# Reordering the input products of two chained MLPs by their weight tiles, with block 0's products cut in two

## The chip, the cores and the metric

The kernel runs on one core of a Trainium2 chip. The metric is the device time of one execution in microseconds (us). Before the change it is 1236.48 us, the median of three runs (1236.11 to 1237.58).

## What is computed

The reference chains three stages over 8192 tokens of width 192: a causal window of 7 neighbours weighted by a softmax, an MLP with SiLU, and an MLP with a rational activation. The changed code is in the first product of each MLP, `h = x @ w_in`.

```python
def _moe_ref(x, w_in, w_out):
    h = x @ w_in                              # 8192x192 by 192x2048
    g = h * (1.0 / (1.0 + np.exp(-h)))
    return (g @ w_out).astype(np.float32)

def _moe2_ref(x, w_in, w_out, a, b):
    h = x @ w_in
    h2 = h * h
    h3 = h2 * h
    P = a[0] + a[1] * h + a[2] * h2 + a[3] * h3
    Q = 1.0 + np.abs(b[0]) * np.abs(h) + np.abs(b[1]) * h2
    g = P / (Q + 1e-06)
    return (g @ w_out).astype(np.float32)
```

## The kernel before

The tokens are handled in 16 blocks `b` of 512 columns. `attention(b)` (line 530) makes the block's input on VectorE (DVE) and GpSimd (POOL), TensorE (PE) transposes it into PSUM, and `split_x` (line 650) splits it into a high and a low part in fp32r: ScalarE (ACT) writes `xh` (line 655), and after it DVE writes `xl` (line 659) as what `xh` left over. Those two steps stand in the plan as `XH0`, `XL0` for the first MLP and `XH1`, `XL1` for the second, whose input is the first one's accumulator (`between`, line 739).

Weights are split in the same way: `WA` holds the first 128 rows of `w_in` as a high and a low tile, `WB` the other 64 rows with high above low. `mm1` (line 667) makes one unit `u` of `h`: two tiles of 128 hidden features (`i` is 0 or 1), each from five products of a 128x128 weight tile with 512 columns of `xh` or `xl`. There are 8 units for each block and MLP, called `A0` to `A7` in the first MLP and `B0` to `B7` in the second, so 256 units and 2560 products. `mm2` (line 691) adds a unit's activation into the accumulator with ten products more (`C0` to `C7`, `D0` to `D7`).

In `mm1` the order is by moving operand: first the three products with `xh` for `i` = 0 and the three for `i` = 1, then the two with `xl` for `i` = 0 and the two for `i` = 1. So the first product that needs `xl` is the seventh of ten.

The order of all steps is a table written by hand (`ORDER`): each engine takes its steps in the order in which they stand there, and a step's engine waits at a single instruction until what it reads has been written. After `mm1`, ACT reads the whole `h` (SiLU in line 723, the linear part in line 768, the magnitude in line 772), so it waits for the last product of a unit. The buffer of `h` is one of four PSUM pairs, marked A to D in the table, and is free for the next unit when the last reader of the former one has ended.

At the start PE runs two warm-up steps without a result: `W0` (line 636) transposes the same 128x128 piece of `xw` 84 times, and `W1` (line 614) the same piece of `ao` 16 times.

Of the kernel before, what the change touches and what calls it, by code (L numbers as in the profile page):

```python
# [20 lines left out]
P = 128  # L21
# [3 lines left out]
BT = JB * P  # L25
# [195 lines left out]
SHARED = {"y", "t", "g1h", "g1l", "g2h", "g2l", "ao", "of", "xh0", "xl0", "xh1", "xl1", "pr"}  # L221
BANKS = {"h", "acc0", "acc1", "dec"}
OWN = dict(xw=1, aw=2)
CHUNKS = (4, 4, 8, 16, 16, 16)
WARM = (84, 16)

# [48 lines left out]
def kernel(  # L275
# [13 lines left out]
    pe, act, dve, pool, sp = nc.tensor, nc.scalar, nc.vector, nc.gpsimd, nc.sync  # L289
# [29 lines left out]
    def new(buf, shape, dt=F32, name=None):  # L319
        if buf[0] in SHARED:  # L320
            return sb.tile(shape, dt, tag="s" + plan.slot[buf], name=name or buf[0], bufs=1)
        return sb.tile(shape, dt, tag=buf[0], name=name or buf[0], bufs=OWN[buf[0]])

    def bank(buf, shape=(P, 2, BT), name=None):
        return ps.tile(list(shape), F32, tag="p" + plan.slot[buf], name=name or buf[0], bufs=1)
# [339 lines left out]
    def mm1(m, b, u):  # L665
        hb = ("h", m, b, u)
        xh, xl = (f"xh{m}", b), (f"xl{m}", b)

        def run(e):
            if hb not in st:  # L670
                st[hb] = bank(hb)
            h, th, tl = st[hb], st[xh], st[xl]
            first = ((WA[m][0], th[:, 0]), (WA[m][1], th[:, 0]), (WB[m], th[:, 1]))
            second = ((WA[m][0], tl[:, 0]), (WB[m], tl[:, 1]))
            for terms in (first, second):
                for i in range(2):
                    f = slice((2 * u + i) * P, (2 * u + i + 1) * P)
                    for n, (w, xx) in enumerate(terms):
                        pe.matmul(  # L679
                            out=h[:, i], lhsT=w[:, f], rhs=xx,  # L680
                            start=(terms is first and n == 0), stop=(terms is second and n == 1),
                        )

        first = [(*hb, 0)] if (m, b, u) == (0, 0, 0) else []
        plan.op(
            f"{'AB'[m]}{u}", b, "PE", run, rd=[*first, (*xh, 0), (*xl, 0), ("W", m, "A", u // 4), ("W", m, "B", u // 4)],
            wr=[(*hb, 0)],
        )
        return hb
# [202 lines left out]
    for m in range(2):  # L892
        for u in range(NU):
# [4 lines left out]
            if u % 2 == 0:  # L898
                weights(m, "O", u // 2)
    for i in range(2, len(CHUNKS)):  # L900
        softmax(f"s{i}", sum(CHUNKS[:i]), CHUNKS[i], False)
    for b in range(NB):
# [43 lines left out]
```

## Time and profile before

| | before |
|---|---|
| median of three runs | 1236.48 us (1236.11 to 1237.58) |
| span of the profiled execution | 1234.3 us |
| outside that span (median less span) | 2.2 us |
| PE, matmuls | 1210.9 us busy, 98% |
| PE, weight loads (PEld) | 1000.2 us busy, 81% |
| ACT | 1107.3 us busy, 90% |
| DVE | 1060.1 us busy, 86% |
| POOL | 704.4 us busy, 57% |

The profile gives no time of its own for the profiled execution beside its span; the 2.2 us are the median of the runs less that span. In the timeline a row has its start and its length in us, the engine, the line of the kernel, the operation, the output and the inputs, and how many instructions it merges; in brackets stands how long the engine sat idle before it and what ended that. Matmuls overlap: a matmul's row is longer than the distance to the next one's start, and this distance, not the length, is what one costs in a stream.

### The profile page before, as it was taken

The numbers are of one execution on the slowest core, as the hardware profiler recorded it, in microseconds if no ns is written. First come the engines' busy times: TensorE is split into PE (matmuls) and PEld (weight loads), VectorE is DVE, ScalarE is ACT, GpSimd is POOL, SyncE is SP. The second block draws the span as 40 slices with busy tenths as digits, with TensorE's granted clock in tenths as the row PEclk, the third lists the DMA queues.
The fourth block names the chain that finished last, engine by engine and source line by source line (L and its number), as shares of the span: only waits on it lengthen the run. The fifth ranks groups of instructions, "written<-read, shape, count | busy, mean of one in ns | idle before, by whom it ended". The sixth has DMA issues, their size and how long they took to land.

```text
span 1234.3 us, 14596 instructions
## 1 busy us (share of the span) xinstructions
PE 1210.9 (98%) x5476; PEld 1000.2 (81%) x5476; DVE 1060.1 (86%) x956; ACT 1107.3 (90%) x1053; POOL 704.4 (57%) x455
## 2 busy tenths in 40 slices
PE   6999999999999999999999999999999999999998
PEld 5777888888888888888888888888888888888786
DVE  8899899898799887898899998787887888878797
ACT  4999999889899999798987998988999899999996
POOL 3758578777654656657446773756727454241531
PEclk8999999999999999999999999999999999999999
DMA  8810010110010100100001020100101000000000
GB/s 245 254 60 33 9 64 9 36 37 25 33 37 3 61 18 1 58 32 25 15 1 54 13 64 1 31 31 1 57 1 54 2 13 9 5 22 1 9 14 26
DMA packets 19230, 45.15 MB, mean 37 GB/s; under 512 B 3932, under 2 KB 10714, under 8 KB 19160
## 3 DMA queue, kind: packets, MB, share of 16 engines
q1 hardware_dynamic: 19160, 44.22, 11.5%
q8 instruction: 43, 0.70, 0.2%
q14 instruction: 27, 0.22, 0.1%
HBM read 31.73 MB, written 7.90 MB: 32 GB/s over the span
## 4 chain that ended last, share of the span: by engine, by line
PE 86%; DVE 6%; ACT 5%; issue 2%; DMA 1%; POOL 1%; SPq 0%; ACTq 0%; DVEq 0%; POOLq 0%
PE h L679 43%; PE acc L710 8%; PE acc L711 8%; PE acc L706 8%; PE acc L708 8%; PE acc L707 8%; ACT L911 1%; PE to L835 1%; DVE y L787 1%; DVE g1l L731 1%; ACT y L792 1%; ACT y L795 1%; ACT y L772 1%; DVE dec L461 1%; DVE t L778 1%
## 5 line engine op out<-in xcount | busy, mean ns | idle before, releaser
L808 POOL TENSOR_TENSOR g2l<-t,g2h 128x1024 fp32r<-128x1024 f32 x95 | 247.5, 2612 | 162.7 <-DVE g2h L317 93.2
L679 PE MATMUL h<-xh,wa 128*128 128x512 f32 x1024 | 317.6, 391 | 4.2 <-DVE g1l L731 1.8
L315 POOL TENSOR_SCALAR g2h<-t 128x1024 fp32r<-128x1024 f32 x84 | 108.8, 1298 | 230.6 <-DVE t L798 207.4
L679 PEld LDWEIGHTS h<-xh,wa 128*128 128x128 f32 x1024 | 190.6, 188 | 48.6 <-issue 3.8
L911 ACT ACT_TABLE_LOAD x167 | 214.3, 1283 | 3.7 <-PEq L930 0.7
L787 DVE SCALAR_TENSOR_TENSOR y<-y,b_sb 128x1024 f32<-128x1024 f32 x128 | 184.6, 1450 | 23.0 <-ACT y L772 22.7
L679 PE MATMUL h<-xl,wa 128*128 128x512 f32 x512 | 199.4, 390 | 0.4 <-DVE xl L659 0.4
L679 PE MATMUL h<-xh,wb 128*128 128x512 f32 x512 | 199.3, 389 | 0.0
L679 PE MATMUL h<-xl,wb 128*128 128x512 f32 x512 | 199.3, 389 | 0.0
L731 DVE TENSOR_TENSOR g1l<-h,g1h 128x1024 fp32r<-128x1024 f32 x128 | 155.6, 1219 | 47.8 <-ACT g1h L727 43.5
L778 DVE TENSOR_TENSOR t<-t,h 128x1024 f32<-128x1024 f32 x128 | 155.2, 1214 | 40.1 <-ACT t L768 26.2
L798 DVE SCALAR_TENSOR_TENSOR t<-t,a_sb,y 128x1024 f32<-128x1024 f32 x128 | 174.3, 1376 | 16.3 <-ACT y L795 16.0
L581 POOL TENSOR_TENSOR pr<-xw,aw 128x768 f32<-128x768 f32 (+1 forms) x99 | 153.0, 1554 | 32.2 <-DMA aw<-wsm 10.9
L781 DVE SCALAR_TENSOR_TENSOR t<-t,a_sb,h 128x1024 f32<-128x1024 f32 x128 | 163.5, 1278 | 8.2 <-ACT y L772 4.9
L723 ACT ACTIVATE h<-h 128x1024 f32<-128x1024 f32 x128 | 129.5, 1012 | 40.2 <-PE h L679 35.0
L768 ACT ACTIVATE t<-h,a_sb 128x1024 f32<-128x1024 f32 x128 | 153.4, 1202 | 13.1 <-PE h L679 12.0
L772 ACT ACTIVATE y<-h,b_sb 128x1024 f32<-128x1024 f32 x128 | 141.9, 1112 | 19.6 <-PE h L679 13.7
L792 ACT ACTIVATE y<-y,c_sb 128x1024 f32<-128x1024 f32 x128 | 144.4, 1148 | 10.4 <-DVE y L787 9.7
L727 ACT ACTIVATE g1h<-h 128x1024 fp32r<-128x1024 f32 x128 | 131.0, 1027 | 6.4 <-PE acc L711 1.3
L795 ACT ACTIVATE y<-y 128x1024 f32<-128x1024 f32 x128 | 131.1, 1054 | 0.6
L679 PEld LDWEIGHTS h<-xl,wa 128*128 128x128 f32 x512 | 96.1, 188 | 20.9 <-DVE xl L659 0.9
L679 PEld LDWEIGHTS h<-xh,wb 128*128 128x128 f32 x512 | 96.2, 188 | 20.3
(96 smaller groups left out, 2249.9 us busy)
## 6 DMA issues: line engine op xcount, KB each, us to landing
xw<-in_x_dram SPq DMA_DIRECT2D x14, 960.0 KB, 4.8
raw<-in_moe_w_out_dram SPq DMA_DIRECT2D x16, 383.5 KB, 7.2
out_dram<-of SPq DMA_DIRECT2D x15, 384.0 KB, 2.6
e<-e SPq DMA_DIRECT2D x32, 128.0 KB, 2.3
raw<-in_moe_w_in_dram SPq DMA_DIRECT2D x8, 511.8 KB, 7.3
raw<-in_moe_w_in_dram SPq DMA_DIRECT2D x8, 255.9 KB, 7.6
aw<-wsm SPq DMA_DIRECT2D x14, 112.0 KB, 3.1
sm<-in_weight_gen_dram SPq DMA_DIRECT2D x3, 448.0 KB, 3.8
```

The source lines that it names most:

```text
L581: e.tensor_tensor(out=p.rearrange("p k (h g) -> p k h g", g=G), in0=st[xw][:, j + k0:j + k0 + n, :].rearrange("p k (h g) -> p k h g", g=G) ...
L679: pe.matmul(out=h[:, i], lhsT=w[:, f], rhs=xx, start=(terms is first and n == 0), stop=(terms is second and n == 1),)
L731: dve.tensor_tensor(out=t, in0=st[hb], in1=st[gh].bitcast(F32), op=ALU.subtract)
L768: act.activation(out=q, in_=st[hb], func=AF.Identity, scale=a_sb[:, 3:4], bias=a_sb[:, 2:3])
L772: act.activation(out=q, in_=st[hb], func=AF.Abs, scale=b_sb[:, 1:2])
L778: dve.tensor_tensor(out=st[t], in0=st[t], in1=flat(), op=ALU.mult)
L781: dve.scalar_tensor_tensor(out=st[t], in0=st[t], scalar=a_sb[:, 1:2], in1=flat(), op0=ALU.add, op1=ALU.mult)
L787: dve.scalar_tensor_tensor(out=st[y], in0=st[y], scalar=b_sb[:, 0:1], in1=st[y], op0=ALU.add, op1=ALU.mult)
L792: act.activation(out=st[y], in_=st[y], func=AF.Ln, scale=c_sb[:, 0:1], bias=1e-6)
L798: dve.scalar_tensor_tensor(out=st[t], in0=st[t], scalar=a_sb[:, 0:1], in1=st[y], op0=ALU.add, op1=ALU.mult)
L808: e.tensor_tensor(out=q, in0=st[t], in1=st[gh].bitcast(F32), op=ALU.subtract)
L911: act.preload_act_table((None, AF.Silu, AF.Ln, AF.Sigmoid, AF.Exp)[k])
```

## The change

Per tile `i` the five products now run in one go, in the order `WA` high with `xh`, `WA` high with `xl`, `WA` low with `xh`, `WB` with `xh`, `WB` with `xl`. The second and the fifth have the weights of the one ahead. In block 0 each product is cut into two of 256 columns, one behind the other with the same weights.

```diff
+PARTS = ((slice(0, BT),), (slice(0, BT // 2), slice(BT // 2, BT)))
...
             first = ((WA[m][0], th[:, 0]), (WA[m][1], th[:, 0]), (WB[m], th[:, 1]))
             second = ((WA[m][0], tl[:, 0]), (WB[m], tl[:, 1]))
-            for terms in (first, second):
-                for i in range(2):
-                    f = slice((2 * u + i) * P, (2 * u + i + 1) * P)
-                    for n, (w, xx) in enumerate(terms):
-                        pe.matmul(
-                            out=h[:, i], lhsT=w[:, f], rhs=xx,
-                            start=(terms is first and n == 0), stop=(terms is second and n == 1),
-                        )
+            terms = (first[0], second[0], first[1], first[2], second[1])
+            for i in range(2):
+                f = slice((2 * u + i) * P, (2 * u + i + 1) * P)
+                for n, (w, xx) in enumerate(terms):
+                    for c in PARTS[b == 0]:
+                        pe.matmul(out=h[:, i, c], lhsT=w[:, f], rhs=xx[:, c], start=(n == 0 and c.start == 0), stop=(n == 4 and c.stop == BT))
```

On PE, unit `B2` of block 8 (the first of the second MLP in that block) stood so before; `wa_73` is the high tile, `wa_74` the low one:

```order
L679 MATMUL h<-xh_5273,wa_73 128x512
L679 MATMUL h<-xh_5273,wa_74 128x512
L679 MATMUL h<-xh_5273,wb_76 128x512
L679 MATMUL h<-xh_5273,wa_73 128x512
L679 MATMUL h<-xh_5273,wa_74 128x512
L679 MATMUL h<-xh_5273,wb_76 128x512
L679 MATMUL h<-xl_5294,wa_73 128x512
L679 MATMUL h<-xl_5294,wb_76 128x512
```

The last two rows come once more, for the second tile. With the change the same place reads:

```order
L681 MATMUL h<-xh_5433,wa_73 128x512
L681 MATMUL h<-xl_5454,wa_73 128x512
L681 MATMUL h<-xh_5433,wa_74 128x512
L681 MATMUL h<-xh_5433,wb_76 128x512
L681 MATMUL h<-xl_5454,wb_76 128x512
```

These five come twice. The first product that reads `xl` moved from the seventh place to the second.

In block 0, unit `A0` now reads, also on PE:

```order
L681 MATMUL h<-xh_284,wa_71 128x256 x2
L681 MATMUL h<-xl_313,wa_71 128x256 x2
L681 MATMUL h<-xh_284,wa_72 128x256 x2
L681 MATMUL h<-xh_284,wb_75 128x256 x2
L681 MATMUL h<-xl_313,wb_75 128x256 x2
```

Where ten products of 512 columns stood there are twenty of 256. No row on the other engines moves.

## Rows read from the trace of the kernel before

**Rows 1.** The page's first part: busy time, share of the span and instructions of each engine.

```profile
PE 1210.9 (98%) x5476; PEld 1000.2 (81%) x5476; DVE 1060.1 (86%) x956; ACT 1107.3 (90%) x1053; POOL 704.4 (57%) x455
```

**Rows 2.** The page's fourth part: the chain that ended last, by engine and by line.

```profile
PE 86%; DVE 6%; ACT 5%; issue 2%; DMA 1%; POOL 1%; SPq 0%; ACTq 0%; DVEq 0%; POOLq 0%
PE h L679 43%; PE acc L710 8%; PE acc L711 8%; PE acc L706 8%; PE acc L708 8%; PE acc L707 8%; ACT L911 1%; PE to L835 1%; DVE y L787 1%; DVE g1l L731 1%; ACT y L792 1%; ACT y L795 1%; ACT y L772 1%; DVE dec L461 1%; DVE t L778 1%
```

**Rows 3.** Busy time by stretch: us, then PE, PEld, DVE, ACT, POOL, clock, DMA.

```profile
28.00:122.00 94.00, 90.43 (x395) 72.09 (x395) 87.69 (x104) 88.72 (x99) 66.47 (x49) 0.99 0.37 119
122.00:1165.00 1043.00, 1042.74 (x4701) 863.25 (x4699) 889.14 (x764) 948.45 (x885) 607.46 (x380) 1.00 0.08 24
1165.00:1235.00 70.00, 62.01 (x280) 49.98 (x278) 60.77 (x58) 58.33 (x56) 20.24 (x10) 0.99 0.07 21
```

**Rows 4.** Who PE waited for from 30 to 122 us: total, times, longest.

```profile
PE h L679 <- ACT xh L655: 0.6, 1, 0.6
PE h L679 <- DVE wa L482: 0.5, 1, 0.5
```

**Rows 5.** Timeline of PE in the middle of the run.

```profile
605.79 0.39 PE L679 MATMUL h<-xh,wb 128*128 128x512 f32 x1
606.02 0.39 PE L679 MATMUL h<-xl,wa 128*128 128x512 f32 x1
```

**Rows 6.** Timeline of the weight loads in the same place.

```profile
605.80 0.19 PEld L679 LDWEIGHTS h<-xl,wa 128*128 128x128 f32 x1
```

**Rows 7.** Groups of instructions by line: step `W0`.

```profile
L636 PE MATMUL tp<-ident,xw 128*128 128x128 f32 x84 | 11.4, 307 | 8.0 <-DMA xw<-in_x_dram 8.0
L636 PEld LDWEIGHTS tp<-ident,xw 128*128 128x128 f32 x84 | 11.2, 162 | 8.0 <-issue 8.0
```

**Rows 8.** Timeline of PE, the later part of `W0`.

```profile
13.81 5.40 PE L636 MATMUL tp<-ident,xw 128*128 128x128 f32 x48
```

**Rows 9.** Timeline of PE: eight transposes of eight different tiles.

```profile
175.71 1.03 PE L835 MATMUL to<-ident,of 128*128 128x128 f32 x8
```

**Rows 10.** Timeline of the weight loads behind an idle stretch of PE.

```profile
177.01 0.30 PEld L679 LDWEIGHTS h<-xh,wa 128*128 128x128 f32 x2 [0.50 <-DVE g1l L731]
```

**Rows 11.** Timeline of DVE and PE, unit `A2` of block 1.

```profile
68.97 1.22 DVE L659 TENSOR_TENSOR xl<-tp,xh 128x1024 fp32r<-128x1024 f32 x1
...
70.25 0.50 PE L679 MATMUL h<-xl,wa 128*128 128x512 f32 x1 [0.45 <-DVE xl L659]
70.59 0.40 PE L679 MATMUL h<-xl,wb 128*128 128x512 f32 x1
```

**Rows 12.** Timeline of DVE and PE, unit `B2` of block 8.

```profile
662.92 1.21 DVE L659 TENSOR_TENSOR xl<-acc,xh 128x1024 fp32r<-128x1024 f32 x1
...
663.17 0.62 PE L679 MATMUL h<-xh,wa 128*128 128x512 f32 x2
```

**Rows 13.** Timeline of DVE and PE, unit `B0` of block 10.

```profile
802.36 1.23 DVE L659 TENSOR_TENSOR xl<-acc,xh 128x1024 fp32r<-128x1024 f32 x1 [0.29 <-ACT xh L655]
...
802.93 0.62 PE L679 MATMUL h<-xh,wa 128*128 128x512 f32 x2
```

**Rows 14.** Timeline of DVE and PE, unit `B2` of block 15.

```profile
1173.09 1.23 DVE L659 TENSOR_TENSOR xl<-acc,xh 128x1024 fp32r<-128x1024 f32 x1
...
1173.11 0.73 PE L679 MATMUL h<-xh,wa 128*128 128x512 f32 x2 [0.76 <-ACT xh L655]
1173.68 0.40 PE L679 MATMUL h<-xh,wb 128*128 128x512 f32 x1
```

**Rows 15.** Timeline of DVE and PE, unit `B0` of block 2.

```profile
211.01 1.21 DVE L659 TENSOR_TENSOR xl<-acc,xh 128x1024 fp32r<-128x1024 f32 x1
...
212.04 0.61 PE L679 MATMUL h<-xh,wa 128*128 128x512 f32 x2
```

**Rows 16.** Timeline of DVE and PE, unit `A1` of block 12.

```profile
873.59 1.22 DVE L659 TENSOR_TENSOR xl<-tp,xh 128x1024 fp32r<-128x1024 f32 x1
...
874.98 0.67 PE L679 MATMUL h<-xh,wa 128*128 128x512 f32 x2
```

## The prediction

> **What bounds the kernel now.** I read the page's first part, then the chain of waits, then busy time by stretch, and last the timelines at the places that the change touches. The first part shows PE at 98%, with ACT and DVE at 90% and 86% [rows 1]; the chain has 86% on PE, 43% of it on `mm1`'s line alone [rows 2]. By stretch this is sharper: from 122 to 1165 us PE is busy for 1042.74 of 1043 us [rows 3]. There it waits for nobody, so whatever lengthens or shortens its stream does so to the end, with no gap to take it up. Before 122 us and after 1165 us PE has gaps: 3.6 us of 94, and 8.0 us of 70 [rows 3].
>
> What one product costs is the distance between starts: 605.79 to 606.02 us, so 0.23 us [rows 5]. I take 0.227, as 1042.74 us over 4701 matmuls with a few transposes among them is near it [rows 3]. Its weight load begins with the start of the product ahead, at 605.80, and has 0.19 us on its row [rows 6]: each load is hidden under the product before it.
>
> **Part 1: repeated weights.** Outside block 0 there are 240 units with four repeats each, 960 products. Do they get cheaper? The nearest row is `W0`, whose 84 transposes all have one and the same 128x128 weight tile. They show 84 loads for 84 matmuls [rows 7], so there a repeat loads again. In its later part 48 of them take 5.40 us; less the last one's own length of about 0.27 that is 5.13 / 47 = 0.109 us each [rows 8]. Eight transposes of eight different tiles take (1.03 - 0.27) / 7 = 0.109 us each [rows 9]. A repeat is neither skipped nor faster. Those are plain fp32 tiles of 128 columns and the products here are fp32r tiles of 512, so this is not proof, but it is the nearest row there is. And since a 512-column product hides its load anyway, a load that became shorter would save nothing by itself. **Taken: 0 us.** Ends: nothing, or the 13 ns of the rival below.
>
> **Part 2: `xl` is needed five places earlier.** Only the first unit of a block and MLP can notice, 32 places. Before, PE had six products (1.36 us) of `xh` ahead of the first one with `xl`; now it has one. The price of a late `xl` follows from unit `A2` of block 1, the one place where PE waits for `xl` already: DVE ends at 68.97 + 1.22 = 70.19, PE's row begins at 70.25, and it is 0.50 long where 0.39 is usual, because its own load could not run ahead [rows 11]. So a late `xl` starts PE's stream again 0.06 + 0.11 = 0.17 us after DVE's end. Place by place, DVE's end + 0.17 against the time at which the second product would have started (the first's start + 0.227):
>
> - `B2`, block 8: 664.13 + 0.17 = 664.30 against 663.40: 0.90 us [rows 12].
> - `B0`, block 10: 803.59 + 0.17 = 803.76 against 803.16: 0.60 us [rows 13].
> - `B0`, block 2: 212.22 + 0.17 = 212.39 against 212.27: 0.12 us [rows 15]. `B0` of block 7 reads alike, 0.12 us.
> - `B2`, block 15: 1174.32 + 0.17 = 1174.49 against about 1173.45 (the first product starts late after a wait, and the third's row at 1173.68 is 0.23 behind the second): 1.04 us [rows 14].
> - `A2`, block 1: PE waits until 70.25 before and after; then it had four products left and now has nine, 5 x 0.227 = 1.13 us [rows 11].
>
> At the other 26 `xl` ends before the load of the second product is issued (the closest is `A1` of block 12: 873.59 + 1.22 = 874.81 against 874.98 [rows 16]), or, in block 0, inside the first pair of products.
>
> The four in the saturated stretch, 0.90 + 0.60 + 0.12 + 0.12 = **1.74 us**, count in full. Behind each, the rest of the unit, ACT's step on it and all of PE's queue come later. The two in the stretches with gaps, 1.13 + 1.04 = 2.17 us, I count at half, **1.09 us**: PE's later gaps there are waits for DVE, ACT and POOL, which in part run on `h` themselves and so come later too. Ends of this part: 0, if DVE catches up, and 3.9 us.
>
> **Part 3: block 0 in halves.** 16 units with ten products make 160 pairs of 256 columns where 160 products of 512 stood. The trace has no 256-column product. The lower end is the 0.109 us of a 128-column matmul [rows 9]: two cost 0.218, less than 0.227, so 160 x -0.009 = -1.4 us. The upper end is a straight line between 128 and 512 columns, 0.109 + (0.227 - 0.109) / 3 = 0.148, so 0.296 a pair and 160 x 0.069 = +11 us. Which is nearer is decided by the load, since every half loads again: behind an idle stretch two loads of this very kind take 0.30 us together with 0.19 for one, so they follow each other by 0.11 us [rows 10]. Half of a 512-column product is 0.1135. I take 0.120: half the columns of a product, with the same 13 ns of overhead as a whole one (0.227 less 0.213, which is an estimate: 512 columns at one for each cycle of the full clock, 2.4 GHz, granted at 1.00 in that stretch [rows 3]). That is 0.240 a pair, +13 ns, 160 x 0.013 = 2.1 us. The 80 pairs of the first MLP run before 60 us, and PE then waits 0.5 us for a weight tile that DVE makes and 0.6 us for ACT's `xh` [rows 4]; those cover their 1.05 us. Of the 80 pairs of the second MLP, nearly all before 122 us, half stays, **0.5 us**.
>
> The Trainium skill's page "TensorE: Matmul & The Clock Gate", section "Back-to-back issue gap", puts a warm product at N / 2.4 + 2.5 ns, 216 ns for 512 columns and 109 ns for 256; the 0.227 us of the rows is above it, and by that rule alone part 3 would be 160 x (0.218 - 0.227) = -1.4 us in place of my 0.5.
>
> **Sum.** 0 + 1.74 + 1.09 + 0.5 = 3.3 us on the span of 1234.3, so 1237.6; with the 2.2 us outside it, **1239.8 us**, 0.27% over the median. A measurement of this kernel can tell about 0.2%, 2.5 us, from no change.
>
> **The rivals.**
>
> *A repeat saves its changeover (faster).* The 13 ns by which a product exceeds 512 cycles may be the price of putting new weights in place. If a repeat doesn't pay it, or its load is left out, 960 x 13 ns = 12.5 us go; with the 2.8 us of part 2 that leaves about 1227 us. It decides as soon as over 5 ns of those 13 go with the weights. For it: the 13 ns are there at every change of weights [rows 5], and this kernel has no repeat among fp32r products to look at. Against it: the 84 equal tiles, which load 84 times at the pace of different ones [rows 7 to 9]. Chance 0.13. The same page, section "Step-by-step: what each phase is for", says that the load is an instruction of its own so that one load can serve many products; no row here shows it done, `W0` shows the contrary.
>
> *The late `xl` is taken up (no change).* If DVE reaches `xl` earlier once PE is behind, or the later gaps absorb it, part 2 is 0 to 1 us and the time 1236.5 to 1237.8. For it: DVE is 85% busy in the saturated stretch (889.14 of 1043 [rows 3]). Against it: `xl` hangs on `xh` and this on PE's own accumulator or transposes, so it comes later with PE. Chance 0.17.
>
> *Halves that cost a load's whole row (slower).* If a half can't start until its load's 0.19 us are over [rows 6], a pair takes 0.38 and 160 pairs 24 us; at the straight line 11 us. As ACT and DVE are 94% and 93% busy there [rows 3], a third to a half of that may be covered: 1243 to 1252 us. Against it: the loads that follow by 0.11 us [rows 10]. Chance 0.08.
>
> That the change doesn't do what it says is excluded by the order of PE's instructions.
>
> **How the numbers follow.** My forecast has 0.62. Its own range is 1237.5 to 1242.5, part 2 from 1 to 3.9 us and part 3 from 0 to 2; about two thirds of it lie over 1239.0, the bound of slower by over 0.2%. Slower: 0.41 + 0.08 = 0.49, taken as 0.50. Same: 0.21 of the forecast and most of the second rival, 0.35. Faster: the first rival and a little of the lower end of part 3, 0.15. The range leaves out the first rival and the dear end of the third: 1234.0 to 1246.0.
>
> **What would show it.** Right: PEld counts 160 loads more and no fewer; in mid-run products still start 0.227 us apart, repeats too; PE waits for `xl` at `B2` of block 8, `B0` of block 10 and `B2` of block 15, with 0.4 to 1 us each; the halves start 0.11 to 0.12 us apart. Wrong: fewer loads than matmuls, repeats 0.213 to 0.216 us apart, halves 0.15 us or more apart, or no wait for `xl` at those places.

## The result and the profile after

The changed kernel takes 1243.97 us, the median of three runs (1242.24 to 1244.07), against 1236.48 us. It is slower: by 7.5 us between the medians, and by 6.7 between the means, whose ratio is 1.0054 with an interval of 1.0034 to 1.0074. The span of the profiled execution is 1242.3 us, 8.0 more than before. Where both are known, a run's time is 1.8 us more than its span (1244.07 and 1242.3), so the profiled execution of before, at 1234.3, was most likely the shortest of its three (1236.11), not the median from which the 2.2 us outside the span were taken; the one after was the longest of its three. That is why the spans are further apart than the medians. The forecast had the sign and less than half of the size: 3.3 us.

The page of the kernel after, busy time of each engine and the chain that ended last:

```profile
PE 1216.1 (98%) x5636; PEld 1010.8 (81%) x5636; DVE 1061.2 (85%) x956; ACT 1106.7 (89%) x1053; POOL 700.5 (56%) x455
...
PE 85%; ACT 6%; DVE 4%; issue 1%; DVEq 0%; ACTq 0%
```

There are 160 matmuls and 160 loads more than in [rows 1], so each of the 5636 products still has a load of its own, the repeats too. The shares of the engines on the chain have hardly moved against [rows 2].

Busy time by stretch, after (us, then PE, PEld, DVE, ACT, POOL, clock, DMA share, GB/s):

```profile
28.00:122.00 94.00, 89.11 (x517) 77.16 (x516) 84.37 (x101) 83.80 (x95) 61.78 (x48) 0.97 0.38 120
122.00:1165.00 1043.00, 1041.79 (x4708) 862.69 (x4707) 886.32 (x762) 945.91 (x883) 602.69 (x380) 1.00 0.08 24
1165.00:1243.00 78.00, 69.23 (x311) 55.71 (x309) 67.78 (x63) 65.09 (x62) 25.80 (x12) 0.99 0.06 19
```

In the first stretch PE is 1.3 us less busy than in [rows 3], although its products are cut finer there, and the granted clock (the share of its full speed that TensorE's clock was given) is 0.97 in place of 0.99. The middle stretch has 0.95 us more idle time.

Whom PE waited for, after (us in total, times, longest):

```profile
PE h L681 <- DVE xl L660: 3.3, 4, 1.6
...
PE h L681 <- DVE t L780: 0.7, 2, 0.5
```

Before, the wait for `xl` happened once, for the 0.45 us of [rows 11]. Now it happens four times.

Timeline of PE after, in the middle of the run. These are five products of one tile, and the columns are those of [rows 5]:

```profile
700.20 0.39 PE L681 MATMUL h<-xh,wa 128*128 128x512 f32 x1
700.42 0.39 PE L681 MATMUL h<-xl,wa 128*128 128x512 f32 x1
700.65 0.39 PE L681 MATMUL h<-xh,wa 128*128 128x512 f32 x1
700.88 0.39 PE L681 MATMUL h<-xh,wb 128*128 128x512 f32 x1
701.10 0.39 PE L681 MATMUL h<-xl,wb 128*128 128x512 f32 x1
```

The second and the fifth have the weights of the one ahead. They start 0.22 us behind it, and the others start 0.23 behind theirs: with two decimals all of them are the 0.227 us of before.

**Where the 8.0 us arise.** The start of a unit's first product, before and after, gives how late PE is. At `A2` of block 1 it is 0.76 us late (68.16, now 68.92). One unit later, at `A1` of block 1, it is 3.25 us late (71.30, now 74.55). At `B1` of block 0 it is 4.18 (98.05, now 102.23), at `B2` of block 8 it is 5.50 (663.17, now 668.67), just behind `B0` of block 10 it is 6.99, at `B2` of block 15 it is 6.92 (1173.11, now 1180.03), and one unit later 7.96 (1175.53, now 1183.49). No more than 0.26 us is gained back between these places (at `A7` of block 1). In each profiled execution in which `B0` of block 2 is late, another 0.12 to 0.17 us are lost ahead of `B5` of block 2, and in none of the others. The largest step by far is one unit, `A2` of block 1, with 2.5 us. Timeline of DVE and PE there, after:

```profile
68.92 0.50 PE L681 MATMUL h<-xh,wa 128*128 128x512 f32 x1 [0.62 <-ACT xh L656]
69.73 1.22 DVE L660 TENSOR_TENSOR xl<-tp,xh 128x1024 fp32r<-128x1024 f32 x1
71.00 0.79 PE L681 MATMUL h<-xl,wa 128*128 128x512 f32 x1 [1.58 <-DVE xl L660]
71.59 0.63 PE L681 MATMUL h<-xh,wa 128*128 128x512 f32 x1
72.02 0.63 PE L681 MATMUL h<-xh,wb 128*128 128x512 f32 x1
```

PE runs one product, waits 1.58 us for `xl`, and then its products start 0.43 us apart, where 0.227 is usual. Busy time in the same place (columns as above):

```profile
69.00:70.00 1.00, 0.43 (x1) 0.11 (x1) 0.90 (x3) 0.50 (x2) 0.00 (x0) 1.00 0.00 0
70.00:71.00 1.00, 0.00 (x0) 0.00 (x0) 1.00 (x2) 1.00 (x2) 0.00 (x0) 0.78 0.46 98
71.00:72.00 1.00, 1.00 (x2) 0.83 (x3) 1.00 (x3) 0.96 (x2) 0.00 (x0) 0.50 0.86 185
72.00:73.00 1.00, 1.00 (x4) 0.78 (x3) 0.91 (x2) 0.00 (x0) 0.00 (x0) 0.50 0.73 168
73.00:74.00 1.00, 1.00 (x4) 0.81 (x3) 0.96 (x2) 0.00 (x0) 0.97 (x1) 0.51 0.94 329
74.00:75.00 1.00, 1.00 (x5) 0.79 (x5) 0.53 (x1) 0.25 (x1) 1.00 (x2) 1.00 0.31 105
```

Behind the idle time the granted clock is 0.50, the lower of its two levels (1.2 GHz), for some 3 us. Before, it was 1.00 throughout this place; one row of it, before:

```profile
71.00:72.00 1.00, 1.00 (x5) 0.69 (x5) 0.91 (x3) 0.71 (x2) 0.00 (x0) 1.00 0.68 168
```

The other late `xl` look as they were forecast. Timeline of DVE and PE after, unit `B2` of block 8:

```profile
668.41 1.22 DVE L660 TENSOR_TENSOR xl<-acc,xh 128x1024 fp32r<-128x1024 f32 x1
668.67 0.40 PE L681 MATMUL h<-xh,wa 128*128 128x512 f32 x1
669.68 0.50 PE L681 MATMUL h<-xl,wa 128*128 128x512 f32 x1 [0.61 <-DVE xl L660]
670.02 0.39 PE L681 MATMUL h<-xh,wa 128*128 128x512 f32 x1
```

DVE ends at 669.63 and the second product's row begins 0.05 us behind it, long by 0.11, as the price from [rows 11] has it. The clock stays at 1.00 there. The unit costs 0.90 us more than before. `B0` of block 10 costs 0.63, `B0` of blocks 2 and 7 cost 0.14 and 0.15, and `B2` of block 15 costs 1.04:

```profile
1180.03 0.50 PE L681 MATMUL h<-xh,wa 128*128 128x512 f32 x1 [0.76 <-ACT xh L656]
1181.29 0.51 PE L681 MATMUL h<-xl,wa 128*128 128x512 f32 x1 [0.76 <-DVE xl L660]
1181.63 0.40 PE L681 MATMUL h<-xh,wa 128*128 128x512 f32 x1
```

Timeline of PE after, halves of block 0 (two in each row):

```profile
102.55 0.40 PE L681 MATMUL h<-xl,wa 128*128 128x256 f32 x2
102.78 0.40 PE L681 MATMUL h<-xh,wa 128*128 128x256 f32 x2
103.02 0.40 PE L681 MATMUL h<-xh,wb 128*128 128x256 f32 x2
103.26 0.40 PE L681 MATMUL h<-xl,wb 128*128 128x256 f32 x2
```

A pair takes 0.24 us, 0.120 for each half, as forecast.

### The profile page after: what moved, and what is told of

It reads as the page before. It is cut to its first block, busy times and chain, and to the rows that moved or that the text cites. A ratio compares the mean times of both kernels' runs of the same rounds, so it can differ in the third digit from the quotient of the medians.

```text
span 1242.3 us, 14916 instructions
## 1 busy us (share of the span) xinstructions
PE 1216.1 (98%) x5636; PEld 1010.8 (81%) x5636; DVE 1061.2 (85%) x956; ACT 1106.7 (89%) x1053; POOL 700.5 (56%) x455
## 3 DMA queue, kind: packets, MB, share of 16 engines
q1 hardware_dynamic: 19160, 44.22, 11.6%
## 4 chain that ended last, share of the span: by engine, by line
PE 85%; ACT 6%; DVE 4%; issue 1%; DVEq 0%; ACTq 0%
PE h L681 43%; PE acc L705 8%; PE acc L709 8%; PE acc L706 8%; PE acc L710 8%; PE acc L707 8%; ACT L910 1%; ACT y L794 1%; PE to L834 1%; DVE g1l L730 1%; ACT y L791 1%; DVE y L786 1%; ACT g1h L726 1%; ACT y L771 1%; ACT h L722 1%
## 5 line engine op out<-in xcount | busy, mean ns | idle before, releaser
L681 PE MATMUL h<-xh,wa 128*128 128x512 f32 (+1 forms) x1088 | 402.8, 380 | 4.3 <-DVE g1l L730 1.8
L681 PEld LDWEIGHTS h<-xh,wa 128*128 128x128 f32 x1088 | 201.6, 189 | 47.4 <-DVE g1l L730 3.2
L681 PE MATMUL h<-xl,wa 128*128 128x512 f32 (+1 forms) x544 | 201.5, 380 | 3.3 <-DVE xl L660 3.3
L681 PE MATMUL h<-xh,wb 128*128 128x512 f32 (+1 forms) x544 | 200.3, 378 | 0.0
L681 PE MATMUL h<-xl,wb 128*128 128x512 f32 (+1 forms) x544 | 200.2, 378 | 0.0
L681 PEld LDWEIGHTS h<-xl,wa 128*128 128x128 f32 x544 | 100.6, 189 | 23.0 <-DVE xl L660 5.2
L681 PEld LDWEIGHTS h<-xh,wb 128*128 128x128 f32 x544 | 100.4, 189 | 19.0
```

The lines of the kernel that those rows point to most:

```text
L681: pe.matmul(out=h[:, i, c], lhsT=w[:, f], rhs=xx[:, c], start=(n == 0 and c.start == 0), stop=(n == 4 and c.stop == BT))
```

## The experiments

The theory after the first look: repeated weights save nothing; each late `xl` moves PE's whole queue; at `A2` of block 1 the wait brings down the clock and so costs double; and the halves cost their 13 ns a pair with no cover. The rivals: that the lost time comes from the halves; that a slower `A2` has another cause than the clock; and that the new order does save something in the middle of the run, which the waits hide.

The runs of one kernel lie 1 to 4 us apart, and those of the old order too (3.3 us in 11 runs of the kernel before, 3.1 in 11 of the halves alone), so a difference of medians is good to about 1 us, and the single places are read from the traces. In the kernels with the new order one part of the spread fits a fall of the clock that some profiled executions show and others do not. The last two experiments take this up.

### The order alone

```diff
-PARTS = ((slice(0, BT),), (slice(0, BT // 2), slice(BT // 2, BT)))
+PARTS = ((slice(0, BT),),) * 2
```

> The new order of the products, block 0's whole again (512 columns). If the late xl is what costs (theory 1), the five late places keep their price as the changed kernel's trace shows it: A2 of block 1 about 2.5 us, B2 of block 8 0.9, B0 of block 10 0.6, B2 of block 15 1.0, two of 0.1, so 5.2 us over the kernel before, some 1241.7, and at least 1240. If the halves are what costs (theory 2), it is within 1.5 us of the kernel before, at most 1238. If repeats themselves were dearer or cheaper (theory 3), products in mid-run would not stand 0.227 us apart.

Measured: 1242.96 us, ratio 1.0054 (1.0042 to 1.0067). In its trace `A2` of block 1 costs 2.60 us, `B0` of blocks 2 and 7 cost 0.15 and 0.14, `B2` of block 8 costs 0.91, `B0` of block 10 costs 0.65 and `B2` of block 15 costs 2.49. In this execution the clock fell at the last of them too, which the expected 1241.7 did not have. Busy time there, order alone:

```profile
1178.00:1179.00 1.00, 0.58 (x2) 0.48 (x3) 1.00 (x3) 0.98 (x2) 0.00 (x0) 0.95 0.00 0
1179.00:1180.00 1.00, 1.00 (x4) 0.75 (x3) 1.00 (x1) 0.57 (x1) 0.89 (x1) 0.50 0.00 0
1180.00:1181.00 1.00, 1.00 (x4) 0.81 (x3) 0.96 (x2) 0.00 (x0) 1.00 (x1) 0.50 0.00 0
```

It follows that the order makes most of the loss, and that the waits, with the same sizes, don't need the halves. The six places add up to 6.94 us, about the whole of this kernel's loss (6.8 us on the median).

### The halves alone

The five products of a tile in the order of before, block 0's in halves. The edit is shown against the changed kernel.

```diff
-            terms = (first[0], second[0], first[1], first[2], second[1])
-            for i in range(2):
...
+            for terms in (first, second):
+                for i in range(2):
+                    f = slice((2 * u + i) * P, (2 * u + i + 1) * P)
+                    for n, (w, xx) in enumerate(terms):
+                        for c in PARTS[b == 0]:
```

> The old order of the products, block 0's in halves of 256 columns. Theory 1: only the halves' own price, 160 x 0.013 = 2.1 us at most, of which the early gaps cover some: 1237.3 to 1238.6, and no drop of TensorE's clock in the first unit of block 1. Theory 2: most of the 7.5 us, 1241 or more. A half stands 0.120 us behind the one ahead, as in the changed kernel.

Measured: 1238.38 us, ratio 1.0019 (1.0010 to 1.0027), so 2.2 us slower; the span is 1236.7, 2.45 more than before. Each unit of block 0 is 0.13 us longer. One wait takes up a little: PE waits for the weight tile ahead of `A5` of block 0, 0.53 us before, and here (timeline of PE, halves alone):

```profile
45.88 0.71 PE L681 MATMUL h<-xh,wa 128*128 128x256 f32 x4 [0.38 <-DVE wa L483]
```

So of the first MLP's 1.04 us PE is 0.79 later at `A2` of block 1 than at `A0` of block 0. From there to `B1` of block 1, where block 0 has ended, it loses 1.75 us, which is 0.7 more than the 1.04 of the second MLP's pairs. 0.6 of that is lost shortly ahead of `B1` of block 0, of which the last section says more. That the whole comes out near 160 x 0.013 is therefore in part chance. The clock did not fall anywhere on PE's way through the blocks.

### The new order, but not in the first unit of a block

Whole products. The first unit of each block and MLP, which alone can be early for `xl`, keeps the order of before; the other 224 units have the new one. The edit is shown against the kernel of the order alone.

```diff
+            begun = (m, b) in seen
+            seen.add((m, b))
...
+            if not begun:
+                for terms in (first, second):
...
+            else:
+                terms = (first[0], second[0], first[1], first[2], second[1])
```

> The new order in all units but the first of each block and MLP, which keeps the old one; block 0's products whole. 896 repeats stay and no product needs xl early. Theory 1: no difference from the kernel before, within 1.5 us (1235 to 1238). If a repeat saved its 13 ns (the first rival of the prediction), 896 x 13 ns = 11.6 us less, about 1225. If repeats cost something, over 1238.

Measured: 1235.96 us, ratio 0.9999 (0.9990 to 1.0008). 896 repeats are in this kernel, and none of the waits. A repeat that saved its 13 ns would have made it 11.6 us faster. So the rival of the saved changeover falls; and as there is no loss either, the whole loss of the order sits in the first units.

### `A2` of block 1 in the order of before

The changed kernel, but for this one unit of 256.

```diff
+            if (m, b, u) == (0, 1, 2):
+                for terms in (first, second):
...
+            else:
+                terms = (first[0], second[0], first[1], first[2], second[1])
```

> The changed kernel with one unit, A2 of block 1, in the old order. Theory 1 with the clock: the 2.5 us that this unit lost (1.13 us by the wait itself, the rest by products at half the clock behind it) come back in full, so about 2.5 us under the changed kernel, 1241.5; TensorE stays at full clock there. If later gaps had taken part of the loss up, under 1.3 us come back. If the clock drop has another cause than the wait for xl, it stays.

Measured: 1241.64 us, ratio 1.0046 (1.0034 to 1.0059), 2.3 us under the changed kernel. In the trace PE's lateness drops by 2.52 us at this unit against the changed kernel. Timeline of PE there:

```profile
70.42 0.49 PE L682 MATMUL h<-xl,wa 128*128 128x512 f32 x1 [0.42 <-DVE xl L660]
70.75 0.39 PE L682 MATMUL h<-xl,wb 128*128 128x512 f32 x1
```

The wait is 0.42 us, as in [rows 11], and the products behind it are at the usual distance. So the 2.5 us hang on this one unit's order. In the profiled execution the clock fell at `B2` of block 15 and cost some 1.5 us there, which the changed kernel's own did not. PE was 0.59 us ahead of the changed kernel when it came to this unit, so its span of 1240.7 is 0.59 + 2.52 - 1.5 = 1.6 below. The 2.3 us of the medians therefore hold more than this unit, and are its price only roughly.

### The five late `xl` of the second MLP in the order of before

```diff
+            if (m, b, u) in ((1, 2, 0), (1, 7, 0), (1, 8, 2), (1, 10, 0), (1, 15, 2)):
+                for terms in (first, second):
...
+            else:
+                terms = (first[0], second[0], first[1], first[2], second[1])
```

> The changed kernel with five units in the old order: B2 of block 8, B0 of blocks 2, 7 and 10, B2 of block 15. Theory 1: their waits for xl go, 0.9 + 0.6 + 0.15 + 0.15 + 1.0 = 2.8 us, and with the last also the chance that the clock falls there; so 2.8 us under the changed kernel, about 1241.2, and no wait for xl but that of A2 of block 1. If DVE's lateness only moved on to another wait, less than 1.4 us come back.

Measured: 1241.0 us, ratio 1.0034 (1.0022 to 1.0046), 3.0 us under the changed kernel. Place by place the trace gives back 0.14, 0.14, 0.88, 0.62 and 1.06, together 2.84 us, and none of it is lost again later. The span is 1239.7. With the experiments before this one the loss is closed. By the traces: 2.45 (halves) + 2.52 (`A2` of block 1) + 2.84 (these five) + 0.14 (what the late `B0` of block 2 loses again ahead of `B5`) = 7.95 of the 8.0 us between the spans. By the medians: 2.2 + 2.3 + 3.0 = 7.5 us, which is closer than their spread allows to count on. The seven times of this kernel go from 1239.13 to 1243.21, two of them at 1239.1 and 1239.4 and four at 1241.0 to 1241.4. Whether the clock held at `A2` of block 1 in the two short ones is not shown, as only a run at 1241.44 was profiled; there it fell.

### Every product in halves

The order of before, all 2560 products cut in two, so that the price of a half is read from 2560 pairs and not from 160. The edit is shown against the kernel of the halves alone.

```diff
-PARTS = ((slice(0, BT),), (slice(0, BT // 2), slice(BT // 2, BT)))
+PARTS = ((slice(0, BT // 2), slice(BT // 2, BT)),) * 2
```

> The old order of the products, all 2560 input products in halves, so 16 times the dose. If a half costs 0.120 us in stream, 2560 x 0.013 = 34 us more than the kernel before, 1270; TensorE's stretch from 122 us on takes nearly all of it, as no gap covers it there. At 0.109 each it would be 23 us faster than before, at a straight line of 0.148 each 177 us slower.

Measured: 1271.4 us, ratio 1.0282 (1.0263 to 1.0300). That is 35.1 us for 2560 pairs, 13.7 ns each. Timeline of PE:

```profile
699.18 0.40 PE L681 MATMUL h<-xl,wa 128*128 128x256 f32 x2
699.42 0.40 PE L681 MATMUL h<-xl,wb 128*128 128x256 f32 x2
```

Products of 256 columns start 0.120 us apart. The Trainium skill's page "TensorE: Matmul & The Clock Gate", section "Back-to-back issue gap", has a formula for an isolated product (N / 2.4 + 2.5 ns) that gives 109 ns for them; two of them would then take less than the 0.227 us of a whole product, and this kernel would have been faster than before. No row here agrees with it for these products, each of which has its own load: the part that does not shrink with the columns is 2 x 0.120 - 0.227 = 0.013 us.

### Block 0 in quarters

The order of before, block 0's products cut in four of 128 columns. Three of four repeat the weights of the one ahead, so this looks again at whether a repeat is cheaper. The edit is shown against the kernel of the halves alone.

```diff
-PARTS = ((slice(0, BT),), (slice(0, BT // 2), slice(BT // 2, BT)))
+PARTS = ((slice(0, BT),), tuple(slice(q * P, (q + 1) * P) for q in range(4)))
```

> The old order, block 0's products in quarters of 128 columns, one behind the other with the same weights. If each one loads its weights again and loads follow each other by 0.108 us, quarters stand 0.108 to 0.111 us apart, 0.435 for a product, 160 x 0.21 = 33 us more busy time, of which the gaps in the early stretch cover some: 1258 to 1270. If a load with the same weights were left out or shortened, a quarter would cost 0.053 + 0.013 = 0.067 us and the time would stay under 1246.

Measured: 1270.1 us, ratio 1.0271 (1.0252 to 1.0290). Timeline of PE, four quarters in each row:

```profile
35.13 0.61 PE L681 MATMUL h<-xh,wb 128*128 128x128 f32 x4
35.58 0.61 PE L681 MATMUL h<-xl,wa 128*128 128x128 f32 x4
36.03 0.61 PE L681 MATMUL h<-xl,wb 128*128 128x128 f32 x4
```

Four take 0.45 us, 0.112 each. At the slope between 512 and 256 columns (0.107 us for 256) a quarter would cost 0.067. It costs what a 128-column matmul with its load costs in [rows 8, 9], 0.109: a repeat is no cheaper. That fits a pace set by the loads, which follow each other by 0.11 us in [rows 10] and have no idle time here (PEld is busy for 9.00 of the 9.00 us from 29 to 38); a floor of the 128-column product itself would look the same and was not told apart from it. 160 products that cost 0.45 instead of 0.227 are 35.7 us, and the kernel lost 33.8: nearly nothing of it was covered.

### The wait at `A2` of block 1 filled

The changed kernel with seven more products of `xh` ahead of the unit's first product with `xl`. They write the second tile, which its own first product overwrites afterwards, so this is extra work and leaves nothing out. PE keeps working while it waits; `xl` comes no earlier.

```diff
                 for n, (w, xx) in enumerate(terms):
+                    if (m, b, u, i, n) == (0, 1, 2, 0, 1):
+                        for _ in range(7):
+                            pe.matmul(out=h[:, 1], lhsT=w[:, f], rhs=th[:, 0], start=True, stop=True)
```

> The changed kernel with seven products more in A2 of block 1 between its first product and the first with xl: they write the second tile, whose own first product overwrites it, and need only xh, so TensorE works through most of the wait for xl. Theory of the clock: the wait itself is as long as before (xl is not earlier), but the granted clock stays at 1.00, the nine products behind it stand 0.227 us apart in place of 0.43, and 1.3 to 1.4 us come back: about 1242.6. If the slow products behind the wait have another cause than TensorE's idleness (DVE, the DMA traffic there), they stay slow and the time is that of the changed kernel or longer.

Measured: 1244.18 us, ratio 1.0056 (1.0043 to 1.0069), the same as the changed kernel. But the place itself changed. Timeline of PE there, and busy time a little behind:

```profile
69.38 1.79 PE L682 MATMUL h<-xh,wa 128*128 128x512 f32 x7
71.12 0.50 PE L684 MATMUL h<-xl,wa 128*128 128x512 f32 x1
71.45 0.39 PE L684 MATMUL h<-xh,wa 128*128 128x512 f32 x1
71.69 0.39 PE L684 MATMUL h<-xh,wb 128*128 128x512 f32 x1
```

```profile
71.00:72.00 1.00, 1.00 (x5) 0.76 (x5) 1.00 (x4) 1.00 (x2) 0.00 (x0) 1.00 0.96 197
...
1181.00:1182.00 1.00, 1.00 (x3) 0.76 (x3) 0.96 (x2) 0.04 (x1) 1.00 (x1) 0.50 0.00 0
```

The first product with `xl` begins 2.08 us behind the unit's first product (69.04 us), as in the changed kernel. Yet the next unit begins at 73.30, so this one takes 4.26 us in place of 5.63 (74.55 - 68.92), at a clock of 1.00 and with products 0.23 apart. Before, it took 3.14 (71.30 - 68.16). So of its 2.5 us, 1.4 were the clock, and 1.1 are left for the order: the 1.13 that the prediction had worked out. The transfers were as busy as in the changed kernel (DMA share 0.96 from 71 to 72 us, 0.86 there), so they are not what made the products slow. The 1.4 did not come out at the end, because in this execution the clock fell at `B2` of block 15 instead (the second row) and cost some 1.5 us. So the expected 1242.6 was missed, by a fall that it did not have. The single times stand in two groups, 1242.3 (two) and 1244.2 to 1244.3 (three), 1.9 us apart; the profiled one is of the upper group.

### Both waits filled

The same, with three extra products at `B2` of block 15 as well.

```diff
+                    if i == 0 and n == 1:
+                        for _ in range({(0, 1, 2): 7, (1, 15, 2): 3}.get((m, b, u), 0)):
+                            pe.matmul(out=h[:, 1], lhsT=w[:, f], rhs=th[:, 0], start=True, stop=True)
```

> As e8_filled_wait, with three products more in the same place of B2 of block 15, which write the second tile ahead of its own first product. Theory of the clock: in e8_filled_wait the slow products were gone in block 1, and the clock fell at B2 of block 15 instead, in some executions and not in others (1242.3 or 1244.2 us). With that wait filled too, all executions lie near 1242.3, within 0.7 us of each other, and the granted clock is 1.00 at both places. If the clock at block 15 falls for another reason, or for the idle time ahead of the unit alone, two groups of times remain, 1.9 us apart.

Measured: 1242.48 us, ratio 1.0051 (1.0037 to 1.0065). All its times lie between 1242.31 and 1243.23. Busy time at the two places:

```profile
70.00:74.00 4.00, 4.00 (x18) 2.99 (x17) 3.88 (x6) 2.54 (x5) 1.38 (x2) 1.00 0.81 219
...
1181.00:1182.00 1.00, 1.00 (x7) 0.79 (x6) 0.96 (x2) 0.00 (x0) 1.00 (x1) 1.00 0.00 0
```

The clock is 1.00 at both, and the span is 1240.5, 1.9 less than with one wait filled. 0.6 of that PE had ahead already at `A2` of block 1; most of the rest is the fall at `B2` of block 15. So a kernel with every wait in its place, but with PE kept busy through the two longest, is 6.3 us slower than before: 4.0 from the six late `xl` (1.13 + 0.14 + 0.15 + 0.90 + 0.63 + 1.04) and 2.2 from the halves. The rest of the changed kernel's 7.5 us is the clock. No version of these beat the kernel before.

## Why the prediction was right, and where it was not

The measured 1243.97 us lie within the whole range, 1234.0 to 1246.0, and the kernel is slower, the verdict that was given the highest chance. They lie above the forecast's own range, 1237.5 to 1242.5: part 2 came to 5.4 us (4.0, and 1.4 of the clock), over its end of 3.9, and part 3 to 2.2, over its end of 2. The upper end of the whole range came from the rival of the dear halves, which did not act, so that the range holds the result is partly luck.

**Repeated weights, 0 us: right.** Loads and matmuls are equal in number, repeats start 0.227 us apart, and 896 of them alone made no difference (0.9999). The row it was taken from, equal 128-column tiles that load each time [rows 7 to 9], held for fp32r tiles of 512.

**The late `xl`, the sizes: right.** Forecast 0.90, 0.60, 0.12, 0.12, 1.04 and 1.13 us [rows 11 to 15]; measured 0.90, 0.63, 0.14, 0.15, 1.04, and 1.1 for the order's own part of the last. Restart cost, DVE's end, and the five places by which the product moved were enough to work it out.

**The late `xl` in stretches with gaps, "I count at half, 1.09 us": wrong.** The full 2.17 us were lost and hardly any came back: with the order alone PE is 2.14 us late at `A1` of block 1 and still 2.03 at `B1` of block 1 (137 us), and in the changed kernel the 1.04 us of `B2` of block 15 are there to the last unit. That fits gaps which are mostly waits for engines that work on PE's own results and so move with it: the wait for `xh`, which is made from PE's transposes, is 0.6 us at `A2` of block 1 in [rows 4] and 0.62 after, although PE came 0.76 us later. The prediction named this and yet took half. That is 1.1 us of the error.

**What the sum did not have: the clock at `A2` of block 1.** The prediction priced that wait at the products that it pushes back and not at what the idle time does to those behind it. PE sat idle for 0.62 us, ran one product, and sat idle for 1.58 us more; then the granted clock was 0.50 and products came 0.43 us apart. The unit in the old order doesn't show it, and the same wait filled with products doesn't either. 1.4 us.

**The halves, "0.120": right; their cover, "0.5 us": wrong.** 0.120 us for each half was measured in block 0 and again over 2560 pairs. But the cover of 1.05 us for the first MLP's pairs and of half for the second's was not there. PE is 0.18 us early at `A0` of block 0 and 0.76 late at `A2` of block 1, so 0.94 of the 1.04 us arrived there, past both waits of [rows 4]; with the halves alone 0.79 did. The second MLP's pairs lost their 1.04 us in full, and 0.7 more around `B1` of block 0, which the prediction had not. The halves by themselves cost 2.2 us on the median (2.45 in the span). 1.7 us of the error.

In all, 3.3 + 1.1 + 1.4 + 1.7 = 7.5 us. In the spans it is 3.3 + 1.1 + 1.4 + 2.0 (the halves at 2.45), and 0.2 for `B5` of block 2 and the sizes: 8.0. Of the rivals, the saved changeover is excluded by the order without its first units, a late `xl` that is taken up by every place's full loss, and the dear halves by 0.120 us.

## What to carry to other kernels

Where a weight load is hidden under the product before it, ordering products by equal weights buys nothing on these rows; look first at which operand comes last, and keep everything that doesn't need it ahead of it. Idle time of the bounding engine covers nothing if it is a wait for work that hangs on that engine's own results: it moves along, so count a delay there in full. And a new wait on TensorE can cost twice: once for what it pushes back, and once at half the clock for the few microseconds behind it. Here that came behind two waits with one product between them, and not behind the single 0.61 us at `B2` of block 8.

## What was unexpected of the hardware

**A short wait can halve the clock, and not always.** Idle stretches of 0.62 and 1.58 us, with one product between them, were followed by some 3 us at 1.2 GHz. At `B2` of block 15, 0.76 us of waiting, one product and 0.76 us more were followed by it in the profiled executions of three kernels (the order alone, `A2` of block 1 in the old order, and one wait filled) and not in that of the changed kernel, although the waits were alike. Filling the waits with products kept the clock at 1.00, so idle time is part of the cause; what else decides it in one execution was not tried and stays open.

**A DVE step that took almost twice as long when it began 0.03 us behind one of POOL.** In block 0, ahead of `B1`, DVE's step on `y` took 1.32 us before the change. Timelines of DVE and POOL there, before (POOL's row holds two steps):

```profile
94.99 1.32 DVE L787 SCALAR_TENSOR_TENSOR y<-y,b_sb 128x1024 f32<-128x1024 f32 x1
...
93.61 4.01 POOL L591 TENSOR_TENSOR pr<-pr 128x576 f32<-128x576 f32 x2 [1.13 <-DVE pr L581]
```

And after, with PE's wait that follows:

```profile
98.41 2.48 DVE L786 SCALAR_TENSOR_TENSOR y<-y,b_sb 128x1024 f32<-128x1024 f32 x1 [0.16 <-ACT y L771]
...
96.80 3.00 POOL L592 TENSOR_TENSOR pr<-pr 128x576 f32<-128x576 f32 x2 [1.14 <-DVE pr L582]
...
102.23 0.48 PE L681 MATMUL h<-xh,wa 128*128 128x256 f32 x2 [0.46 <-DVE t L780]
```

POOL's two steps are quicker by 1.0 us (3.00 for 4.01), and DVE's one is longer by 1.16. Before, DVE's step ran first and POOL's second one took 2.42 us; after, POOL's second one began at 98.38, took 1.43, and DVE's, 0.03 us behind it, took 2.48. DVE had waited 0.16 us for ACT, which by the trace came later with PE's longer units of block 0. The step takes 2.3 to 2.5 us in all seven kernels with block 0 in halves, and 1.32 or 1.33 in the three with whole products there. In all seven it ends 1.08 or 1.09 us after POOL's step does, also where it began 0.19 us behind it (every product in halves, 2.32 us). The Trainium skill's page "SBUF — State Buffer", section "Who interferes with whom", says that a DVE step with two inputs in SBUF and a GpSimd step share a pair of ports, which the one that starts first holds to the end. The rows agree: 2.48 against 1.32 us. What this costs at the end was not tried by itself; the 0.6 us that the halves lose ahead of `B1` of block 0, beyond their own price, stand in the same place, and PE's wait of 0.46 us there is for the DVE step that comes right behind this one.

**Quarters cost almost as much as halves.** 128-column products with a load each start 0.112 us apart, hardly less than the 0.120 of 256 columns.
